# Gated scan with expert routing on one core: which queue issues the loads of gates and inputs

## The chip, the cores and the metric

The kernel runs on one core of one Trainium2 chip. The metric is the device time of one execution in microseconds (us), taken as the median of several runs. All times of single instructions below come from one profiled execution, counted from the start of its span.

## What is computed

Four sequences of 3648 tokens with 256 channels are first run through a gated linear recurrence. Each token's result then goes to one of 16 experts, chosen in two steps (a group of four, then one of its four experts), and comes back weighted. Cut to what matters:

```python
sig = 1.0 / (1.0 + np.exp(-f_logit))
f = lower_bound + (1.0 - lower_bound) * sig
h = f * h + (1.0 - f) * x[:, t]            # one step per token, h starts at 0 in each sequence
# x is now the 14592 x 256 matrix of all h
g_idx = np.argmax(x @ w_group, axis=1)     # softmax weight g_w of the winner
e_idx = np.argmax(x @ w_expert[g], axis=1) # within the group, softmax weight e_w
out = (g_w * e_w)[:, None] * (np.maximum(x @ w1[g, e], 0) @ w2[g, e])
```

## The kernel before

**Two kinds of work share the core.** The first is the scan with the routing. It goes over 29 units of 512 tokens (unit 0 to unit 28; the last has 256). For a unit the kernel loads gates and inputs in one transfer of 1 MB into a tile `zt` (`p1_load`, L157 to L170), takes the tanh on ACT (L179) and two scaled copies (L183), one product on DVE (L196) and two scans on DVE (L207). PE transposes the result (L226), computes the router's scores (L238) and transposes these (L249). DVE then finds expert and place of every token (`route_thunks`, L252 to L329; units go through it in groups of two after unit 0), with a small matmul for the counts (L284, L285) whose result DVE reads (L310). POOL scatters the tokens' rows into per-expert lists in memory (`xs`, L322).

The second is the experts' matmuls, in jobs: 16 early ones on the first tokens of each expert, 16 later ones on the rest. A job loads its tokens' rows (`xr`, L607), four pieces of weights of 512 KB (`st`, L615, five buffers), splits each piece into a 16-bit high part on ACT (`wh`, L621) and a low part on DVE (`wl`, L622), transposes the rows on PE (L636; high part L641 on ACT, low part L642 on DVE), and does the two layers on PE (L666 to L668, then L681 to L683) with the activation on ACT and DVE in between (L671, L672), a scaled copy on ACT (L687) and a scatter on POOL (L688).

**What sets the order.** The program writes both kinds of work interleaved: the scan's steps are put among a job's matmul steps so that each is done by the time that a later job is due. SyncE's queue (SP in the profile) keeps the order in which the program is written: it issues the loads of units, of rows and of weights and blank rows into the lists (L421), and each of these may wait in front of all that stand behind it. The rows of a job wait for the scatters that fill its list (L607) and for its position, which DVE computes (`posA`, L430, read by L596); a load of weights waits until one of the five buffers is free, that is for an earlier piece's L622. The other engines' orders come from a scheduler, which places each instruction by its own estimate of when it can start. All engines work through their queues in order.

**Where the loads of units stand.** The step of unit u writes the load of unit u+2, then the tanh of unit u+1 (L363). A tile `zt` has four buffers, so the load of unit u also waits for the scans of unit u-4.

```python
zt = p1.tile([P, 2, KD, UNIT], F32, name="zt", bufs=4)
seq += [lambda u=u: (p1_load(u + AHEAD - 1), u + 1 in us and p1_ta(u + 1), early_blanks(u + 4))]
```

Of the kernel before, what the change touches and what calls it, by code (L numbers as in the profile page):

```python
# [32 lines left out]
O_BUFS = 5  # L33
X_BUFS = 4
AHEAD = 3


@with_exitstack
def gated_scan_moe(ctx: ExitStack, tc, zx, lower, wroute, wexp, out, S):
    nc = tc.nc  # L40
# [101 lines left out]
    def unit_range(u):  # L142
        return u * UNIT, min(N, (u + 1) * UNIT)
# [11 lines left out]
    last_load = {}  # L155

    def p1_load(u):  # L157
        if u >= NU:
            return
        a, b = unit_range(u)  # L160
        w = b - a
        zt = p1.tile([P, 2, KD, UNIT], F32, name="zt", bufs=4)
        src = zx[u * P:(u + 1) * P, :].rearrange("p (s k w) -> p s k w", s=2, k=KD)
        if u == 0:
            for k in range(KD):
                for q in range(2):
                    nc.sync.dma_start(out=zt[:, q, k, 0:w], in_=src[:, q, k, 0:w])
        else:
            last_load[u] = nc.sync.dma_start(out=zt[:, :, :, 0:w], in_=src[:, :, :, 0:w])
        units[u] = {"z": zt}  # L170

    def p1_ta(u):
        a, b = unit_range(u)
        w = b - a
        U = units[u]
        U["h"] = p1.tile([P, KD, UNIT], F32, name="h", bufs=3)
        ff = U["z"][:, 0]
        if u > 0:
            nc.scalar.activation(ff[:, :, 0:w], U["z"][:, 0, :, 0:w], AF.Tanh, scale=0.5)  # L179
        for k in range(KD):  # L180
            if u == 0:
                nc.scalar.activation(ff[:, k, 0:w], U["z"][:, 0, k, 0:w], AF.Tanh, scale=0.5)
            nc.scalar.activation(ff[:, k, 0:w], ff[:, k, 0:w], AF.Identity, scale=hlf[:, k:k + 1],  # L183
                                 bias=cen[:, k:k + 1])
        U["f"] = ff
# [145 lines left out]
    def p1_thunks(us, groups):  # L331
# [21 lines left out]
        def put(f):  # L353
            th.append(f or (lambda: None))
            if hasattr(f, "mark"):
                marks[f.mark] = len(th)

        put(lambda: [p1_load(u) for u in range(us[0], us[0] + AHEAD - 1)])
        put(lambda: p1_ta(us[0]))
        for u in us + [us[-1] + 1]:  # L360
            seq = []
            if u in us:
                seq += [lambda u=u: (p1_load(u + AHEAD - 1), u + 1 in us and p1_ta(u + 1), early_blanks(u + 4))]  # L363
            if u - 1 in us:
# [52 lines left out]
    def early_blanks(u):  # L417
        for e, (v, n) in enumerate(EARLY):
            if v == u:
                r = e * LW + PRE - n * P  # L420
                sync.dma_start(out=xs_v[NT + e][r:r + n * P, :].rearrange("(p k) c -> p k c", k=n),  # L421
                               in_=blank[:, None, :].broadcast_to([P, n, RW]))
# [462 lines left out]
```

## Time and profile before

| what | value |
|---|---|
| median of 3 runs | 883.24 us (876.09 to 884.25) |
| profiled execution | 878.25 us |
| its span | 876.5 us |
| mean granted clock of TensorE in the span | 0.934 of full speed |
| PE busy | 753.8 us (86%) |
| DVE busy | 535.7 us (61%) |
| ACT busy | 464.2 us (53%) |
| POOL busy | 286.9 us (33%) |

PE is the engine of the matmuls, DVE the vector, ACT the scalar and POOL the general engine; SP only issues transfers. A profiled execution is 1.75 us longer than its span. Busy shares are means over the whole span, in which a first part (scan and early jobs together, up to some 390 us) and a second part (jobs alone) follow each other. In a timeline a row's bracket says how long the engine had been idle before the instruction and what ended the wait.

### The profile page before, as it was taken

What the parts mean: (1) busy time and instruction counts of PE and PEld (TensorE: products, weight loads), DVE (VectorE), ACT (ScalarE), POOL (GpSimd) and SP (SyncE); (2) the same over time, 40 slices, a digit from 0 to 9 for tenths busy, and PEclk for the clock granted to TensorE, in tenths of its full rate; (3) what the DMA queues carried; (4) which work ended last, traced back from release to release, by engine and by line L of the source; (5) the groups of instructions that cost most, each with busy time, mean ns of one, the idle gap of its engine ahead of it and who ended that gap; (6) DMA issues with size and microseconds to landing.
All of it is one profiled execution on the core that took longest, in us unless ns stands there. A gap on an engine that the chain in (4) does not pass through costs nothing.

```text
span 876.5 us, 17542 instructions
## 1 busy us (share of the span) xinstructions
PE 753.8 (86%) x6629; PEld 646.5 (74%) x6629; DVE 535.7 (61%) x1159; ACT 464.2 (53%) x808; POOL 286.9 (33%) x255
## 2 busy tenths in 40 slices
PE   3452869878887888897799999999999999999995
PEld 2231748756676776766599998999888999999895
DVE  7996959888965953672534454543656445555630
ACT  6763949588745644342545444544555445555531
POOL 0484554734634425541121121212221221112122
PEclk9665979979999989999799999999999999999998
DMA  8993999799897244247641632343543424444300
GB/s 309 273 362 124 304 295 360 225 354 323 279 255 256 101 162 161 100 163 200 223 151 43 217 105 71 105 129 90 144 138 98 122 94 150 146 151 135 126 24 22
DMA packets 59056, 155.34 MB, mean 177 GB/s; under 512 B 11179, under 2 KB 24560, under 8 KB 55515
## 3 DMA queue, kind: packets, MB, share of 16 engines
q1 hardware_dynamic: 44443, 124.12, 44.3%
q0 software_dynamic: 14240, 30.06, 9.8%
q8 instruction: 52, 0.85, 0.4%
q14 instruction: 33, 0.27, 0.1%
q10 hardware_dynamic: 288, 0.03, 0.0%
HBM read 112.65 MB, written 42.05 MB: 176 GB/s over the span
## 4 chain that ended last, share of the span: by engine, by line
PE 56%; issue 11%; DVE 9%; DMA 7%; ACT 4%; SPq 2%; POOL 2%; POOLq 0%; another core or an unknown queue 0%; DVEq 0%; ACTq 0%
PE ps_m L683 9%; PE ps_m L681 9%; PE ps_m L682 9%; PE ps_m L666 8%; PE ps_m L668 8%; PE ps_m L667 8%; DMA st<-in_wexp_dram 5%; DVE wl L622 3%; PE ps_p L636 2%; DVE hl L672 2%; ACT wh L621 2%; POOL out_dram L688 1%; SPq L488 1%; PE ps_p L238 1%; DVE h L207 1%
## 5 line engine op out<-in xcount | busy, mean ns | idle before, releaser
L688 POOL DMA_INDIRECT out_dram<-o,meta x123 | 140.9, 1146 | 472.9 <-ACT o L687 441.2
L681 PE MATMUL ps_m<-wh,hh 128*128 128x256 f16 (+6 forms) x984 | 272.6, 277 | 2.0 <-ACT o L687 1.1
L682 PE MATMUL ps_m<-wl,hh 128*128 128x256 bf16 (+6 forms) x984 | 272.4, 277 | 0.8 <-issue 0.8
L683 PE MATMUL ps_m<-wh,hl 128*128 128x256 f16 (+6 forms) x984 | 272.2, 277 | 0.9 <-issue 0.9
L666 PE MATMUL ps_m<-xh,wh 128*128 128x256 f16 (+12 forms) x896 | 252.7, 283 | 19.8 <-DVE hl L672 19.3
L672 DVE SCALAR_TENSOR_TENSOR hl<-ps_m,hh 128x512 bf16<-128x512 f32 (+11 forms) x270 | 166.1, 620 | 168.7 <-ACT hh L671 128.2
L668 PE MATMUL ps_m<-xh,wl 128*128 128x256 f16 (+12 forms) x896 | 252.4, 283 | 0.2 <-issue 0.2
L667 PE MATMUL ps_m<-xl,wh 128*128 128x256 bf16 (+12 forms) x896 | 252.4, 283 | 0.0
L671 ACT ACTIVATE hh<-ps_m 128x512 f16<-128x512 f32 (+11 forms) x270 | 146.7, 546 | 129.2 <-PE ps_m L668 112.1
L622 DVE TENSOR_TENSOR wl<-st,wh 128x1024 bf16<-128x1024 f32 x128 | 155.4, 1219 | 57.7 <-ACT wh L621 57.5
L322 POOL DMA_INDIRECT xs<-rows,posi x114 | 143.8, 1262 | 110.6 <-issue 27.7
L621 ACT CAST wh<-st 128x1024 f16<-128x1024 f32 x128 | 132.8, 1044 | 43.3 <-DMA st<-in_wexp_dram 22.8
L687 ACT ACTIVATE o<-ps_m,meta 128x256 f32<-128x256 f32 (+6 forms) x123 | 58.3, 474 | 159.5 <-PE ps_m L683 137.7
L681 PEld LDWEIGHTS <-hh 128*128 128x128 f16 (+6 forms) x984 | 112.5, 114 | 12.0 <-issue 4.1
L683 PEld LDWEIGHTS <-hl 128*128 128x128 bf16 (+6 forms) x984 | 112.4, 114 | 10.1 <-issue 2.3
L682 PEld LDWEIGHTS <-hh 128*128 128x128 f16 (+6 forms) x984 | 112.5, 114 | 9.4 <-issue 1.4
L667 PEld LDWEIGHTS <-wh 128*128 128x128 f16 x896 | 88.9, 99 | 38.0 <-issue 22.7
L666 PEld LDWEIGHTS <-wh 128*128 128x128 f16 x896 | 89.0, 99 | 19.1 <-issue 2.7
L668 PEld LDWEIGHTS <-wl 128*128 128x128 bf16 x896 | 88.8, 99 | 19.1 <-issue 1.7
L642 DVE TENSOR_TENSOR xl<-ps_p,xh 128x512 bf16<-128x512 f32 (+9 forms) x68 | 41.9, 617 | 65.1 <-ACT xh L641 64.5
L207 DVE TENSOR_TENSOR_SCAN h<-zt,h 128x512 f32<-128x512 f32 (+4 forms) x56 | 65.1, 1170 | 1.6 <-PE ps_p L226 1.4
L636 PE MATMUL ps_p<-ident,xr 128*128 128x128 f32 (+6 forms) x246 | 40.0, 284 | 30.0 <-DMA xr<-xs 22.0
(120 smaller groups left out, 506.4 us busy)
## 6 DMA issues: line engine op xcount, KB each, us to landing
st<-in_wexp_dram SPq DMA_DIRECT2D x128, 512.0 KB
zt<-in_zx_dram SPq DMA_DIRECT2D x27, 1024.0 KB
xr<-xs SPq DMA_DIRECT2D x31, 258.0 KB
xs<-blank SPq DMA_DIRECT2D x22, 258.0 KB
xr<-xs SPq DMA_DIRECT2D x8, 249.9 KB
out_dram<-o,meta POOLq DMA_INDIRECT x123
xs<-rows,posi POOLq DMA_INDIRECT x114
xs<-blank SPq DMA_DIRECT2D x3, 516.0 KB
```

What stands on the lines that cost most here:

```text
L322: sc = nc.gpsimd.indirect_dma_start(out=xs_v[G["t0"] + t][:, :], out_offset=bass.IndirectOffsetOnAxis(ap=R["posi"][:, t:t + 1], axis=0), i ...
L621: nc.scalar.copy(j.wh[i], j.st[i])
L622: nc.vector.tensor_tensor(out=j.wl[i], in0=j.st[i], in1=j.wh[i], op=ALU.subtract)
L666: nc.tensor.matmul(po, w1_at(j.wh, k, c), xh[:, k], start=(k == 0), stop=False)
L667: nc.tensor.matmul(po, w1_at(j.wh, k, c), xl[:, k], start=False, stop=False)
L668: nc.tensor.matmul(po, w1_at(j.wl, k, c), xh[:, k], start=False, stop=(k == KD - 1))
L671: nc.scalar.activation(hi, pv, AF.Relu)
L672: nc.vector.scalar_tensor_tensor(out=j.hl[ch][:, cs[0]:cs[-1] + 1, 0:w], in0=pv, scalar=0.0, in1=hi, op0=ALU.max, op1=ALU.subtract)
L681: nc.tensor.matmul(pm[0:p, 0:D], j.hh[ch][:, c, ts], w2_at(j.wh, c), start=(c == 0), stop=False)
L682: nc.tensor.matmul(pm[0:p, 0:D], j.hh[ch][:, c, ts], w2_at(j.wl, c), start=False, stop=False)
L683: nc.tensor.matmul(pm[0:p, 0:D], j.hl[ch][:, c, ts], w2_at(j.wh, c), start=False, stop=(c == KF - 1))
L688: nc.gpsimd.indirect_dma_start(out=out_v[out_n[0]][:, :], out_offset=bass.IndirectOffsetOnAxis(ap=lt[0:p, r, 0:1], axis=0), in_=o[0:p], in ...
```

## The change

Loads of unit 0 to unit 8 stay where they were; the loads of units 9 to 28 (20 transfers, nineteen of 1 MB and one of 512 KB) are issued from ACT's queue.

```diff
--- before.py
+++ after.py
@@ -33,6 +33,7 @@
 O_BUFS = 5
 X_BUFS = 4
 AHEAD = 3
+ZX_SP = 9
@@ -166,7 +167,7 @@
         else:
-            last_load[u] = nc.sync.dma_start(out=zt[:, :, :, 0:w], in_=src[:, :, :, 0:w])
+            last_load[u] = (nc.sync if u < ZX_SP else nc.scalar).dma_start(out=zt[:, :, :, 0:w], in_=src[:, :, :, 0:w])
```

Lines of the changed program are one higher (L170 is L169 before). On SP the other instructions keep their order; on ACT, DVE and PE the scheduler comes to another one.

The first place is SP's queue before and after one of the last groups of weights; `zt_3402` is unit 25, `zt_3569` unit 26, `xr` are a job's rows, `st` weights, `posA` a job's position. Before:

```order
L607 DMA xr_3291<-xs 128x516
L169 DMA zt_3402<-in_zx_dram 128x2048
L421 DMA xs<-blank_154 768x1x258 x2
L615 DMA st_3440<-in_wexp_dram 128x1024
L615 DMA st_3482<-in_wexp_dram 128x1024
L615 DMA st_3532<-in_wexp_dram 128x1024
L615 DMA st_3563<-in_wexp_dram 128x1024
L169 DMA zt_3569<-in_zx_dram 128x2048
L596 TENSOR_LOAD posA_3515
L596 ISA x2
L607 ISA
L607 DMA xr_3753<-xs 128x516
```

In the changed program the same stretch of SP reads:

```order
L608 DMA xr_3291<-xs 128x516
L422 DMA xs<-blank_154 768x1x258 x2
L616 DMA st_3440<-in_wexp_dram 128x1024
L616 DMA st_3482<-in_wexp_dram 128x1024
L616 DMA st_3532<-in_wexp_dram 128x1024
L616 DMA st_3563<-in_wexp_dram 128x1024
L597 TENSOR_LOAD posA_3515
L597 ISA x2
L608 ISA
L608 DMA xr_3753<-xs 128x516
```

The two loads of units are gone from between rows, blanks and weights.

The second place is ACT's queue around the end of one early job (`o` and `hh` are its results and activations, `ex` and `Lg` belong to the routing); `wh0_3963` and `wh1_3996` are pieces of the job whose weights are `st_3440` and `st_3482` above, `wh2_3534` and `wh3_3565` are pieces of the job ahead of it. Before:

```order
L687 ACTIVATE o_3319<-ps_m2_3294,meta_2649 128x256
L287 ACTIVATE ex_3327<-ge_3154 128x160
L250 COPY Lg_3329<-ps_p_3330 128x80
L687 ACTIVATE o_3358<-ps_m2_3333,meta_2649 128x256
L621 CAST wh0_3963<-st_3440 128x1024
L621 CAST wh2_3534<-st_3165 128x1024
L621 CAST wh1_3996<-st_3482 128x1024
L687 ACTIVATE o_3397<-ps_m2_3372,meta_2668 128x256
L621 CAST wh3_3565<-st_3193 128x1024
L671 ACTIVATE hh_3423<-ps_m1_3425 128x2x256
```

In the changed program the same place, with the load of unit 25 and the tanh of unit 24 (`zt_3131`):

```order
L170 DMA zt_3402<-in_zx_dram 128x2048
L672 ACTIVATE hh_3114<-ps_m1_3271 128x384
L688 ACTIVATE o_3319<-ps_m2_3294,meta_2649 128x256
L288 ACTIVATE ex_3327<-ge_3154 128x160
L251 COPY Lg_3329<-ps_p_3330 128x80
L688 ACTIVATE o_3358<-ps_m2_3333,meta_2649 128x256
L180 ACTIVATE zt_3131<-zt_3131 128x1024
L622 CAST wh0_3442<-st_3125 128x1024
L184 ACTIVATE zt_3131<-zt_3131,mid_85,half_83 128x512
L688 ACTIVATE o_3397<-ps_m2_3372,meta_2668 128x256
L184 ACTIVATE zt_3131<-zt_3131,mid_85,half_83 128x512
L672 ACTIVATE hh_3423<-ps_m1_3425 128x2x256
```

The load of a unit stands a few rows ahead of the tanh of the unit before it, and the casts of `st_3440` and `st_3482` have moved from here to behind the casts of all earlier pieces; in this part of the queue the casts now stand in the order of their loads, while before three of them stood ahead of older ones.

The third place is DVE's queue at the first early job's rows; `base` is the read of the routing's counts (group of units 7 and 8), `wl_886` to `wl_938` are the low parts of the first five pieces of weights, `scn` belongs to the routing, `h` to a scan. Before:

```order
L277 SCALAR_TENSOR_TENSOR scn<-rmask_403,oh_842 128x128
L196 SCALAR_TENSOR_TENSOR zt<-zt 128x1024
L207 SCALAR_TENSOR_TENSOR h<-zt,h 128x512 x2
L310 TENSOR_TENSOR base<-ps_p,runoff 128x16
L312 TENSOR_TENSOR runoff<-ps_p,runoff 128x16
L315 TENSOR_TENSOR sc<-scn,base 128x128
L642 TENSOR_TENSOR xl<-ps_p,xh 128x2x256
L644 COPY meta<-xr 128x4
```

In the changed program:

```order
L278 SCALAR_TENSOR_TENSOR scn<-rmask_403,oh_842 128x128
L197 SCALAR_TENSOR_TENSOR zt<-zt 128x1024
L311 TENSOR_TENSOR base<-ps_p,runoff 128x16
L313 TENSOR_TENSOR runoff<-ps_p,runoff 128x16
L316 TENSOR_TENSOR sc<-scn,base 128x128
L623 TENSOR_TENSOR wl_886<-st,wh_885 128x1024
L623 TENSOR_TENSOR wl_892<-st,wh_891 128x1024
L623 TENSOR_TENSOR wl_898<-st,wh_897 128x1024
L623 TENSOR_TENSOR wl_904<-st,wh_903 128x1024
L643 TENSOR_TENSOR xl<-ps_p,xh 128x2x256
L645 COPY meta<-xr 128x4
L623 TENSOR_TENSOR wl_938<-st,wh_937 128x1024
```

The five low parts, which stood some 30 to 40 rows ahead of this read, now stand behind it; so do one unit's product (unit 12) and four scans (units 11 and 12).

## Rows read from the trace of the kernel before

**Rows 1.** Windows of 50 and 200 us: busy us (instructions) of each engine, PEclk, DMA share, GB/s

```profile
250.00:300.00 50.00, 38.92 (x356) 32.41 (x355) 33.09 (x71) 29.14 (x53) 20.70 (x16) 0.93 0.68 204
500.00:700.00 200.00, 199.09 (x1759) 179.99 (x1758) 102.42 (x189) 94.80 (x168) 46.41 (x38) 1.00 0.37 113
```

**Rows 2.** Timeline of PE: start us, us, engine, line, what [idle before, releaser]

```profile
128.76 0.19 PE L284 MATMUL ps_p<-scn,tri 128*128 128x16 bf16 x1 [3.12 <-DVE scn L277]
...
181.54 0.69 PE L636 MATMUL ps_p<-ident,xr 128*128 128x128 f32 x2 [8.05 <-ACT rs L241]
...
253.13 0.27 PE L681 MATMUL ps_m<-wh,hh 128*128 128x256 f16 x1 [1.08 <-ACT o L687]
...
266.01 0.48 PE L249 MATMUL ps_p<-ident,rs 128*128 128x128 f32 x1 [4.62 <-ACT rs L241]
...
286.26 0.19 PE L284 MATMUL ps_p<-scn,tri 128*128 128x16 bf16 x1 [4.02 <-DVE xl L642]
```

**Rows 3.** Timeline of ACT, the tanh of units 18, 19, 25, 26, 27, and three casts

```profile
157.58 1.05 ACT L179 ACTIVATE zt<-zt 128x1024 f32<-128x1024 f32 x1
...
175.34 1.06 ACT L179 ACTIVATE zt<-zt 128x1024 f32<-128x1024 f32 x1 [3.68 <-DMA zt<-in_zx_dram]
...
249.88 1.06 ACT L179 ACTIVATE zt<-zt 128x1024 f32<-128x1024 f32 x1 [3.71 <-DMA zt<-in_zx_dram]
...
260.08 2.94 ACT L621 CAST wh<-st 128x1024 f16<-128x1024 f32 x3 [6.29 <-DMA st<-in_wexp_dram]
...
271.13 1.06 ACT L179 ACTIVATE zt<-zt 128x1024 f32<-128x1024 f32 x1 [4.07 <-DMA zt<-in_zx_dram]
...
281.74 1.06 ACT L179 ACTIVATE zt<-zt 128x1024 f32<-128x1024 f32 x1 [6.35 <-DMA zt<-in_zx_dram]
```

**Rows 4.** Timeline of SP's queue, loads of units 19, 26, 27 and of weights

```profile
163.89 0.42 SPq L169 DMA_DIRECT2D zt<-in_zx_dram  x1
...
243.48 19.26 SPq L615 DMA_DIRECT2D st<-in_wexp_dram  x4
262.79 0.42 SPq L169 DMA_DIRECT2D zt<-in_zx_dram  x1
...
275.98 0.42 SPq L169 DMA_DIRECT2D zt<-in_zx_dram  x1
```

**Rows 5.** Chain that ended last, in order of time: start us, us, what

```profile
165.13 13.96 DMA st<-in_wexp_dram
```

**Rows 6.** Windows of 5 us and less, columns as in rows 1

```profile
155.00:160.00 5.00, 5.00 (x59) 4.29 (x58) 5.00 (x13) 3.74 (x7) 4.09 (x4) 1.00 0.26 96
175.00:180.00 5.00, 0.00 (x0) 0.00 (x0) 3.08 (x6) 3.43 (x5) 3.89 (x4) 0.72 1.03 355
180.00:185.00 5.00, 3.46 (x18) 2.61 (x19) 3.78 (x6) 4.17 (x8) 0.00 (x0) 0.50 1.02 411
265.00:270.00 5.00, 3.99 (x21) 2.99 (x22) 5.00 (x7) 2.06 (x6) 4.09 (x4) 0.66 0.94 353
...
286.20:290.00 3.80, 2.91 (x15) 1.87 (x14) 3.74 (x6) 3.80 (x9) 1.74 (x2) 0.55 0.55 164
```

**Rows 7.** Lines L169 and L82: duration in ns, min/median/max, of one issue

```profile
L169 SPq DMA_DIRECT2D zt<-in_zx_dram x28: 327/424/1407, 2.6 to 277.9; - x28
L82 ACTq DMA_DIRECT2D wr<-in_wroute_dram x1: 473/473/473, 1.2 to 1.2; - x1
```

**Rows 8.** Timeline of DVE around the first early job

```profile
55.03 1.21 DVE L622 TENSOR_TENSOR wl<-st,wh 128x1024 bf16<-128x1024 f32 x1
...
78.43 2.46 DVE L207 TENSOR_TENSOR_SCAN h<-zt,h 128x512 f32<-128x512 f32 x2
85.26 0.17 DVE L310 TENSOR_TENSOR base<-ps_p,runoff 128x16 f32<-128x16 f32 x1 [4.37 <-PE ps_p L285]
...
116.31 0.69 DVE L642 TENSOR_TENSOR xl<-ps_p,xh 128x512 bf16<-128x512 f32 x1 [5.08 <-ACT xh L641]
...
127.14 1.23 DVE L196 SCALAR_TENSOR_TENSOR zt<-zt 128x1024 f32<-128x1024 f32 x1 [5.02 <-ACT zt L183]
```

## The prediction

> **What bounds the kernel now.** I read four views in this order: windows by stage, the timeline of PE for its idle times, the timelines of ACT and SP for what ended them, and the chain of waits at the worst place. The windows show two kernels in one. From 500 to 700 us PE is busy 199.09 of 200 us at full clock, and nothing but PE's own work sets the time there; from 250 to 300 us, where scan and early jobs run together, it is busy 38.92 of 50 us at a clock of 0.93 [rows 1]. PE's order from the middle of that part on is the same in both programs, so what PE gains before some 300 us should arrive at the end nearly whole, and the change touches nothing later.
>
> The reader is then to look for the idle times of PE in that part. Five of them matter here [rows 2]: 3.12 us at 128.76, 8.05 at 181.54, 1.08 at 253.13, 4.62 at 266.01 and 4.02 at 286.26. After a longer one the granted clock is low (0.50 from 180 to 185, 0.66 from 265 to 270, 0.55 from 286.2 to 290) [rows 6], so each costs more than its length: what PE was busy there times one minus the clock.
>
> The timeline of ACT says what they waited for [rows 3]. The tanh of units 19, 25, 26 and 27 stood 3.68, 3.71, 4.07 and 6.35 us for their loads, and three casts in a row at 260.08 stood 6.29 us for weights. SP's queue says why those loads were late [rows 4]: unit 26 was issued at 262.79, right behind four loads of weights that took SP 19.26 us to get rid of because they wait for free buffers, and unit 27 at 275.98, behind the rows of a job that wait for scatters.
>
> **The change part by part.** SP loses 20 issues of 0.42 us [rows 7]; it mostly waits, so this alone is worth nothing. ACT gains 20, and each now leaves a few rows ahead of the tanh of the unit before.
>
> *Casts at 260.08.* The first of these is `wh0_3963`, whose weights SP began to issue at 243.48 [rows 4]; it belongs to the job after the next one, yet stands in ACT's queue ahead of a piece that PE needs sooner. ACT held the routing's copy `rs` back for it, and PE stood 4.62 us [rows 2]. In the changed order this cast comes later and those in its place have weights loaded earlier. Gain 4.62 + 3.99 x 0.34 = 6.0 us [rows 2, 6]. Bounds: nothing, if another wait fills the place, and 6.0. I take 6.0, since the order alone removes it.
>
> *Unit 27.* Its load will leave ahead of the tanh of unit 26, which without its own wait can start at 271.13 - 4.07 = 267.1. It took 281.74 - 275.98 = 5.8 us from issue to tanh, so it lands at 272.9; ACT asks for it at 281.74 - 6.35 = 275.4 [rows 3, 4]. Covered by 2.5 us, the wait goes, and with it PE's 4.02 us and 2.91 x 0.45 = 1.3 us of clock: 5.3 us [rows 2, 6]. Bounds 0 and 5.3. I take 5.3. The load of unit 26 leaves ahead of the tanh of unit 25 (249.88 - 3.71 = 246.2, 16.6 us sooner), and that of unit 25 sooner too: PE's 1.08 us at 253.13 goes as well.
>
> *Unit 19.* PE's 8.05 us do not end with the tanh but with the cast behind it, whose weights were issued at 165.13 and took 13.96 us [rows 5]; unit 19's 1 MB stood right ahead of them (163.89) [rows 4]. It will leave ahead of the tanh of unit 18, at about 157.6 [rows 3], where the transfer engines are busy only 0.26 [rows 6]. 1 MB less in front at 355 GB/s is 3.0 us. Bounds: nothing, if unit 20's load takes its place beside the weights, and 8.05 + 3.46 x 0.5 = 9.8 us if the whole stall goes. I take 3.0; the 3.68 us of the tanh lie under the weights' wait. The weights are late next.
>
> *ACT's own cost.* 20 x 0.47 us (the nearest row of an issue by ACT, of a small transfer) = 9.4 us of ACT's queue [rows 7]. ACT is busy 29.14 of 50 us in the first row of rows 1, so much of this falls into its waits. Behind an issue stand a tanh and the activations that PE's next products need. Bounds 0 and 9.4; I take 2, for a fifth of it, as PE is idle in about a fifth of that window.
>
> *First early job.* The five low parts, one product and four scans come to stand behind DVE's read at 85.26, which waits for PE [rows 8]: 5 x 1.21 + 1.23 + 2 x 2.46 = 12.2 us of DVE work put off. The cover is DVE's later idling, 5.08 us before 116.31 and 5.02 before 127.14 [rows 8]. Left over: 12.2 - 10.1 = 2.1 us. The first job's products wait for the first four parts, 4 x 1.21 = 4.8 us, but the second pair of jobs waits for its rows anyway. Bounds: a gain of 3.1 (the stall at 128.76, where the count now stands ahead of the next unit's product on DVE, goes and nothing is left over) and a loss of 12.2. I take a loss of 2.1.
>
> Sum: -6.0 - 5.3 - 1.1 - 3.0 + 2.0 + 2.1 = -11.3 us. Against the profiled execution this is 878.25 - 11.3 = 867.0 us. The runs' median, 883.24, lies 5.0 above that execution, which gives 871.9; I forecast 869, the middle of the two. Rivals below are put on the same middle, 880.7 for no change.
>
> A rule speaks against all this. The Trainium skill's page "DMA: Bandwidth & Descriptors", in "Issuing engines are not separate DMA queues", says that transfers of all issuing engines run on the same 16 engines and that spreading them saves only issue time, small beside the transfer. By it the terms of units 19 and 27 would be zero, which is the first rival. The rows of SP agree on the size of an issue (0.42 us) but show a load held 19.26 us by its place in the queue, which that sentence leaves out.
>
> **The rivals.** *No change that can be seen.* The transfer engines are the limit: from 175 to 185 us they are busy 1.03 and 1.02 of the time [rows 6], and a unit that leaves sooner only delays the weights. Then the terms of units 19, 25 and 27 go, and 6.0 of the casts less 4.1 of costs remain: 880.7 - 1.9 = 879. Against it: the share is 0.26 at 155 to 160, so there is room in which to go sooner [rows 6].
>
> *Slower.* The bound in the first part is the in-order pair ACT and DVE. From 85 us on DVE carries the 12.2 us put off and ACT the 9.4 us of issues; the scatters, and so the rows of every early job, come later by both. Nothing removes it but the 6.0 of the casts: 880.7 + 12.2 + 9.4 - 6.0 = 896. It decides if DVE does not idle between 105 and 130 us any more and is still behind at 130; it turns into a loss once the two costs pass the 15.4 us of the gains. For it: the five parts stand right in front of the first products. Against: the 10.1 us of idle time that DVE has there [rows 8].
>
> *More.* The stall at 181.54 goes whole (9.8 instead of 3.0) and the one at 128.76 too (gain 3.1 instead of a loss of 2.1): 869 - 6.8 - 5.2 = 857. For it: both waits hang on units whose loads now leave by themselves. Against: the weights at 165.13 have more than 1 MB ahead of them.
>
> **How the numbers follow.** Forecast 0.48, no change 0.23, slower 0.15, more 0.14. A difference of 1%, 8.8 us, is about what a measurement can tell from none; it lies at 871.9. The forecast's own range is 862 to 876 (about half of the gains more or less), of which some seven tenths lie below: 0.34. Faster by over 1%: 0.34 + 0.14 = 0.48. Within 1%: 0.14 of the forecast and 0.22 of the first rival: 0.36. Slower: 0.15 and 0.01 of that rival: 0.16. The range is 853 to 890: it leaves out the end of the third rival and most of the second.
>
> **What would show it.** Right: PE's idle times at the places of 253, 266 and 286 us gone, the tanh of units 25 to 27 without waits, three casts no longer in a row behind 6 us of waiting, the low clock after them gone; the first products of the first job about 5 us later, and DVE without its waits of 5 us near 116 and 127. Wrong: casts waiting for weights as long as the tanh did before (the first rival), or the second pair's rows, which DVE takes at 116.31 [rows 8], more than 6 us later and the lead still lost at 200 us (the second). The forecast fails altogether if ACT's issues wait long in its queue, because everything behind them then waits too.

## The result, and the profile after

| what | before | after |
|---|---|---|
| median | 880.28 us (4 runs, 876.09 to 884.25) | 854.32 us (4 runs, 852.42 to 854.65) |
| profiled execution | 878.25 us | 852.42 us |
| granted clock, whole span | 0.934 | 0.951 |
| PE busy | 753.8 us | 742.5 us |

The medians are 26.0 us apart, and the ratio is 0.9686 with an interval of 0.9656 to 0.9715. The prediction had said 869 us, 11.3 us less: the direction was right, the size less than half. Beside other kernels on other chips the changed kernel came to 0.9727 and 0.9695.

The windows of after, with the columns of [rows 1]. The stretch from 200 to 250 us of before was not shown yet and stands ahead.

Before:

```profile
200.00:250.00 50.00, 43.29 (x351) 31.57 (x349) 45.86 (x89) 35.82 (x65) 23.95 (x18) 0.97 0.87 296
```

After:

```profile
200.00:250.00 50.00, 49.20 (x423) 37.82 (x422) 48.91 (x102) 39.45 (x73) 27.34 (x23) 1.00 0.96 299
250.00:300.00 50.00, 48.07 (x476) 41.41 (x473) 40.94 (x84) 31.66 (x58) 22.83 (x19) 1.00 0.71 247
300.00:350.00 50.00, 40.66 (x335) 32.72 (x336) 29.69 (x92) 21.85 (x44) 27.43 (x26) 0.90 0.38 125
500.00:700.00 200.00, 199.09 (x1761) 180.74 (x1759) 103.95 (x186) 96.78 (x170) 44.95 (x37) 1.00 0.37 112
```

From 500 to 700 us nothing has changed, as foreseen. From 200 to 300 us PE stood idle 100 - 43.29 - 38.92 = 17.8 us and now 100 - 49.20 - 48.07 = 2.7 us, and its clock rose from 0.97 and 0.93 to full.

SP's queue gives the lead of the changed kernel at points that both programs reach: each row is the issue of a job's rows (`xr`). Before:

```profile
161.05 1.84 SPq L607 DMA_DIRECT2D xr<-xs  x2
...
211.81 0.92 SPq L607 DMA_DIRECT2D xr<-xs  x2
...
274.16 1.77 SPq L607 DMA_DIRECT2D xr<-xs  x2
...
312.30 1.53 SPq L607 DMA_DIRECT2D xr<-xs  x3
...
384.44 3.93 SPq L607 DMA_DIRECT2D xr<-xs  x6
```

After, the same jobs:

```profile
158.08 0.89 SPq L608 DMA_DIRECT2D xr<-xs  x2
...
207.95 1.26 SPq L608 DMA_DIRECT2D xr<-xs  x2
...
261.53 0.95 SPq L608 DMA_DIRECT2D xr<-xs  x2
...
290.78 1.26 SPq L608 DMA_DIRECT2D xr<-xs  x3
...
357.48 4.22 SPq L608 DMA_DIRECT2D xr<-xs  x6
```

The lead is 3.0, 3.9, 12.6, 21.5 and 27.0 us. So, by these rows, 17.7 of the 25.8 us between the two profiled executions arise between 210 and 310 us.

PE's idle times of [rows 2] are gone or small. So is one of 6.74 us that [rows 2] does not list. Before:

```profile
114.57 1.08 PE L636 MATMUL ps_p<-ident,xr 128*128 128x128 f32 x4 [6.74 <-DMA xr<-xs]
```

The timeline of PE after, at this place, at 181 us, at its first idle time of over 1 us behind 200 us, and at the end of the first part:

```profile
114.88 0.63 PE L637 MATMUL ps_p<-ident,xr 128*128 128x128 f32 x4 [0.84 <-DMA xr<-xs]
...
180.12 0.44 PE L637 MATMUL ps_p<-ident,xr 128*128 128x128 f32 x2 [1.11 <-ACT rs L242]
...
302.00 0.33 PE L250 MATMUL ps_p<-ident,rs 128*128 128x128 f32 x1 [2.11 <-ACT rs L242]
...
395.37 0.48 PE L667 MATMUL ps_m<-xh,wh 128*128 128x384 f16 x1 [14.48 <-DVE hl L673]
```

The 8.05 us at 181.54 are 1.11, and between 200 and 300 us nothing over 1 us is left. The last row is not new, but it is 4.5 us longer than its counterpart before and takes so much of the lead back:

```profile
421.11 0.48 PE L666 MATMUL ps_m<-xh,wh 128*128 128x384 f16 x1 [9.94 <-DVE hl L672]
```

ACT after, with the load of unit 26 and the tanh of units 25, 26 and 27, which answer to [rows 3], and the longest wait of a cast there:

```profile
246.55 0.33 ACTq L170 DMA_DIRECT2D zt<-in_zx_dram  x1
248.01 1.08 ACT L180 ACTIVATE zt<-zt 128x1024 f32<-128x1024 f32 x1
...
259.46 1.06 ACT L180 ACTIVATE zt<-zt 128x1024 f32<-128x1024 f32 x1
...
268.23 1.10 ACT L180 ACTIVATE zt<-zt 128x1024 f32<-128x1024 f32 x1
...
298.09 1.04 ACT L622 CAST wh<-st 128x1024 f16<-128x1024 f32 x1 [8.67 <-DMA st<-in_wexp_dram]
```

None of these three waits, and the three casts behind 6.29 us are gone. Up to here every sign that the prediction had named for the casts and for units 25 to 27 is there. Only the experiments show that the causes it gave were mostly the wrong ones.

### The profile page after: what moved, and what is told of

The parts are those of the page before. It is cut to its first block, busy times and chain, and to the rows that moved or that the text cites. A ratio compares the mean times of both kernels' runs of the same rounds, so it can differ in the third digit from the quotient of the medians.

```text
span 850.3 us, 17541 instructions
## 1 busy us (share of the span) xinstructions
PE 742.5 (87%) x6629; PEld 639.9 (75%) x6629; DVE 539.9 (63%) x1159; ACT 459.8 (54%) x808; POOL 283.1 (33%) x255
## 4 chain that ended last, share of the span: by engine, by line
PE 54%; issue 12%; DVE 8%; DMA 8%; ACT 3%; POOL 3%; SPq 2%; POOLq 0%; another core or an unknown queue 0%; DVEq 0%; ACTq 0%
PE ps_m L683 9%; PE ps_m L682 9%; PE ps_m L684 9%; PE ps_m L667 8%; PE ps_m L669 8%; PE ps_m L668 8%; DMA st<-in_wexp_dram 5%; DVE wl L623 2%; PE ps_p L637 2%; POOL out_dram L689 2%; DVE h L208 1%; POOL xs L323 1%; SPq L489 1%; DMA xs<-rows,posi 1%; ACT wh L622 1%
## 5 line engine op out<-in xcount | busy, mean ns | idle before, releaser
L682 PE MATMUL ps_m<-wh,hh 128*128 128x256 f16 (+6 forms) x984 | 269.6, 274 | 3.0 <-issue 1.8
L683 PE MATMUL ps_m<-wl,hh 128*128 128x256 bf16 (+6 forms) x984 | 269.6, 274 | 0.9 <-issue 0.6
L323 POOL DMA_INDIRECT xs<-rows,posi x114 | 139.6, 1224 | 131.3 <-issue 27.8
L682 PEld LDWEIGHTS <-hh 128*128 128x128 f16 (+6 forms) x984 | 111.4, 113 | 13.1 <-issue 4.4
L227 PE MATMUL ps_p<-ident,h 128*128 128x128 f32 x228 | 43.9, 321 | 12.2 <-DVE h L208 11.4
```

The costliest lines, as they stand in the source:

```text
L323: sc = nc.gpsimd.indirect_dma_start(out=xs_v[G["t0"] + t][:, :], out_offset=bass.IndirectOffsetOnAxis(ap=R["posi"][:, t:t + 1], axis=0), i ...
L682: nc.tensor.matmul(pm[0:p, 0:D], j.hh[ch][:, c, ts], w2_at(j.wh, c), start=(c == 0), stop=False)
L683: nc.tensor.matmul(pm[0:p, 0:D], j.hh[ch][:, c, ts], w2_at(j.wl, c), start=False, stop=False)
```

## The experiments

The change does two things at once: it moves 20 loads to another queue, and it makes the scheduler write ACT, DVE, PE and POOL in another order. To part them, a kernel can be given any order of both programs. When all is written, each instruction of an engine is tied to the one ahead of it in a table, for issue order alone (in short):

```diff
+    for eng, names in ORDER.items():
+        last = None
+        for n in names:
+            i = traced.get(n)
+            if last is not None:
+                tc.add_manual_dep(i, last.name, NoSync, reason="order")
+            last = i
```

The tables are read from the built programs. With this, *order alone* has all loads on SP and the other engines in the order of after; *queue alone* has the loads on ACT and all else in the order of before. Two more give the stage. No run pins an unchanged order; *casts_alone* below, at 1.0009, is the nearest to one. Each run has one profile, and the only one of before comes from the first group of runs, so a difference of a few us between before and an experiment in single windows or waits may be that of two chips. Times and ratios are against before in the same group.

```diff
 late_units:   ZX_SP = 19
 early_units:  (nc.scalar if 9 <= u < 19 else nc.sync)
```

> All loads of units stay on SP's queue at their places of before; the order of ACT, DVE, PE and POOL is pinned to that of the changed program. Queue theory (the gain comes from the loads leaving SP's queue): within 1% of before, 872 to 889 us. Order theory (the gain comes from the scheduler's other order): 850 to 860 us. The prediction's own split, 6.0 us for the casts by order and 2.1 lost on the first job: 876 us.

> The loads of units 9 to 28 go to ACT's queue, while ACT (but for the loads), DVE, PE and POOL keep the order of before, the three casts ahead of older ones included. Queue theory: 850 to 862 us. Order theory: 875 us or more. If both parts are needed together: between, 862 to 875 us.

> Only the loads of units 19 to 28 go to ACT's queue. By the times at which jobs' rows are issued in the two traces the lead is 3.0 us at 158 us, where unit 19 is loaded, and 27.0 us in the end: if each load earns its part where it stands, this one has 24 of the 27.7 us, 856 us. If the gain is an even share per load (10 of 20), 866 us. If relief of the first part is what all rests on, 875 us or more.

> Only the loads of units 9 to 18 go to ACT's queue. Lead by place: 3 to 4 us, 876 us. Even share per load: 866 us. If all rests on the first part: 857 us or less. A loss (over 884 us) if ACT's issues and the first job's order cost more than they bring.

| run | time, us | ratio to before | interval |
|---|---|---|---|
| order_alone | 857.23 | 0.9784 | 0.9711 to 0.9858 |
| queue_alone | 871.57 | 0.9939 | 0.9904 to 0.9974 |
| late_units | 853.69 | 0.9757 | 0.9677 to 0.9837 |
| early_units | 887.73 | 1.0171 | 1.0103 to 1.0240 |

(before 876.55 us in these.) The order brings most without one load moved, and the queue little without the new order. The change to units from 19 on carries the gain; loads of units 9 to 18 on ACT with the rest left on SP, in the order that the scheduler then makes, cost 11 us between the medians (1.0 to 2.4%). In that kernel the tanh of units 22 to 28 have only 43, 51, 54, 60, 68, 71 and 73 activations of jobs ahead of them on ACT, and stand 23.3 us for their loads from 200 to 330 us. What ACT waited for from 100 to 330 us tells why the queue alone is not enough (columns: us in all, times, longest). Before:

```profile
ACT zt L179 <- DMA zt<-in_zx_dram: 18.3, 5, 6.3
...
ACT wh L621 <- DMA st<-in_wexp_dram: 10.5, 4, 6.3
```

Queue alone:

```profile
ACT wh L622 <- DMA st<-in_wexp_dram: 20.2, 10, 6.3
```

The tanh no longer waits for loads at all, and the casts wait for weights longer, 20.2 us against 10.5: of 28.8 us of ACT's waits in these two rows 20.2 are left. That is the first rival's picture.

**Casts out of turn.** The prediction had taken 6.0 us for the casts at 260.08, two of which (`wh0_3963`, `wh1_3996`) stand ahead of older ones; an earlier cast does so too. In *casts_alone* these three and their low parts trade places so that all stand in the order of their loads; nothing else moves (7 places on ACT, 7 on DVE). On ACT, for instance:

```
 L687 ACTIVATE o_3358<-ps_m2_3333,meta_2649 128x256
+L621 CAST wh2_3534<-st_3165 128x1024
+L621 CAST wh3_3565<-st_3193 128x1024
 L621 CAST wh0_3963<-st_3440 128x1024
-L621 CAST wh2_3534<-st_3165 128x1024
+L687 ACTIVATE o_3397<-ps_m2_3372,meta_2668 128x256
 L621 CAST wh1_3996<-st_3482 128x1024
-L687 ACTIVATE o_3397<-ps_m2_3372,meta_2668 128x256
-L621 CAST wh3_3565<-st_3193 128x1024
```

*after_inverted* does the reverse in the changed kernel, *casts_queue* adds the loads on ACT to casts_alone.

> Before, every engine in its own order of before, all loads on SP's queue; only the three casts that stand ahead of older ones (and their low parts) change places with these, so that casts and low parts stand in the order of their loads: 7 places on ACT and 7 on DVE. Theory casts (these three places carry most of what order alone brought, 0.978): 0.975 to 0.985 of before. The prediction's term, 6.0 us: 0.993. Theory rest (routing ahead of the next unit's work, the first job's low parts, PE's order carry it): 0.99 to 1.00.

> After, with the 20 loads on ACT's queue and every engine in its order of after; only casts and low parts stand in the mutual order of before again (the same 7 places on ACT and on DVE). Theory casts: the gain falls from 27 us to about 8, ratio 0.985 to 1.00. The prediction's term: 0.969 + 6.0 us = 0.975. Theory rest: 0.97 or less.

> Before's order on all engines but for the casts and low parts in the order of their loads, and the loads of units 9 to 28 on ACT's queue: the two parts together without the rest of the new order. If casts (0.978) and queue (0.994) add up and nothing else matters: 0.97 to 0.975, like after. If the rest of the order carries the gain: 0.985 to 0.995.

> The changed kernel once more, beside the three others on one chip: 0.966 to 0.972 of before.

| run | time, us | ratio to before | interval |
|---|---|---|---|
| casts_alone | 863.76 | 1.0009 | 0.9979 to 1.0038 |
| after_inverted | 848.16 | 0.9821 | 0.9785 to 0.9858 |
| casts_queue | 855.34 | 0.9910 | 0.9880 to 0.9941 |
| after_again | 839.75 | 0.9727 | 0.9690 to 0.9764 |

(before 863.77 us.) In the order of before the places of the three casts are worth nothing; in that of after the same places cost 848.16 - 839.75 = 8.4 us. The waits of ACT in casts_alone from 200 to 330 us show what came in their place:

```profile
ACT zt L179 <- DMA zt<-in_zx_dram: 21.9, 3, 10.6
```

Before, the same row of the same stretch had 14.1 us:

```profile
ACT zt L179 <- DMA zt<-in_zx_dram: 14.1, 3, 6.3
```

The wait moved from the casts to the tanh. So the theory that these casts carry the order's gain falls.

**Which part of the order.** *late_order* has the order of before up to 168 us and that of after from there on. The three others keep the order of before and move one class of instructions to where after has it, as far as the order of all pairs on which both programs agree is kept. All loads stay on SP.

> All loads on SP's queue. Every engine stands in its order of before up to the first cast behind which unit 19 was loaded (168 us in the trace of before), and in its order of after from there on. Theory late order: the later part alone carries what order brings, ratio 0.975 to 0.985. Theory first job (low parts and scans put off at 85 us fill DVE's idle time from 100 to 150 us, and all rests on that): 0.995 or more. Half and half: 0.988.

> All loads on SP's queue, orders of before; only the units' own work (tanh and scaled copies on ACT, product and scans on DVE) stands among the rest where after has it, as far as the dependences both orders share allow; it mostly comes later. Theory units (they ran ahead of what was due and stood in front of it): 0.978 to 0.987. Else 0.995 to 1.005; and over 1.005 if late scans hold up PE's transposes.

> All loads on SP's queue, orders of before; only the routing's steps (maxima, places, positions and rows on DVE, the exponential on ACT, the counts on PE) stand among the rest where after has them; they mostly come earlier. Theory routing (positions and rows sooner, so the next jobs' rows are loaded sooner): 0.978 to 0.987. Else 0.995 to 1.005.

> All loads on SP's queue, orders of before; only casts on ACT and low parts on DVE stand among the rest where after has them: in the order of their loads, mostly later and one by one between the activations of a job instead of in bursts. Theory spread casts (a burst of casts and low parts stands in front of activations that PE waits for): 0.978 to 0.987. Else 0.995 to 1.005, as the mere change of places gave 1.001.

| run | time, us | ratio to before | interval |
|---|---|---|---|
| late_order | 859.45 | 0.9754 | 0.9704 to 0.9804 |
| units_moved | 866.25 | 0.9838 | 0.9784 to 0.9891 |
| routing_moved | 877.65 | 0.9945 | 0.9909 to 0.9980 |
| casts_moved | 890.78 | 1.0102 | 1.0070 to 1.0135 |

(before 882.33 us.) The later part of the order carries all of its gain, as far as the intervals tell (0.9754 here, 0.9784 for the whole order). Within it the units' own work is the largest piece that was tried, routing a small one, and the new places of the casts cost time by themselves.

**Which units, and the queue once more.** *last_eight* moves only the own work of units 21 to 28, *order_again* repeats order_alone beside the changed kernel, and *after_old_casts* puts the casts of the changed kernel where before has them. In last_eight ACT's order changes like this around the tanh of unit 23 (`zt_2908`; `hh` and `o` belong to a job):

```
-L179 ACTIVATE zt_2908<-zt_2908 128x1024
-L183 ACTIVATE zt_2908<-zt_2908,mid_85,half_83 128x512 x2
 L687 ACTIVATE o_3068<-ps_m2_3043,meta_2363 128x256
 L228 COPY rows_2944<-ps_p_3073 128x2x256
+L687 ACTIVATE o_3104<-ps_m2_3079,meta_2370 128x256
+L250 COPY Lg_2875<-ps_p_3111 128x80
+L671 ACTIVATE hh_3114<-ps_m1_3116 128x384
+L179 ACTIVATE zt_2908<-zt_2908 128x1024
```

> The order of after with all loads on SP's queue, once more, beside the changed kernel on one chip. If the queue adds what it gave to the order of before (0.994) or to that with casts in place (0.990): 0.975 to 0.98 of before here, and the changed kernel 5 to 9 us less. If the queue adds nothing once the order is right: the two alike within 3 us.

> The changed kernel, for comparison with order_again: 0.967 to 0.973 of before.

> All loads on SP's queue, orders of before; only the own work of units 21 to 28 (tanh, scaled copies, product, scans) stands where after has it. On ACT the tanh of units 22 to 28 then have 49, 56, 64, 70, 73, 78 and 80 activations of jobs ahead of them instead of 45, 53, 56, 62, 69, 71 and 73. Theory late units (ACT asked for the last loads too early and stood): 0.980 to 0.988, what all units moved gave. If the earlier units carry it: 0.995 or more.

> The changed kernel with 20 loads on ACT's queue and its order, but casts and low parts standing among the rest where before has them, out of turn ones included, as far as the dependences both orders share allow. Moved alone, the new places of casts cost 1.0%. If that adds up: 0.957 to 0.965, better than both. As the out-of-turn casts cost the changed kernel 1.0% (after_inverted), it may cancel: 0.97. If casts must stand late where the units do: 0.98 or more.

| run | time, us | ratio to before | interval |
|---|---|---|---|
| order_again | 841.76 | 0.9744 | 0.9704 to 0.9784 |
| after_third | 837.68 | 0.9695 | 0.9657 to 0.9734 |
| last_eight | 851.57 | 0.9861 | 0.9819 to 0.9902 |
| after_old_casts | 844.66 | 0.9783 | 0.9743 to 0.9823 |

(before 864.88 us.) On one chip the order brings 864.88 - 841.76 = 23.1 us and the queue on top of it 841.76 - 837.68 = 4.1 us. Eight units, moved behind 1 to 8 more activations of jobs, bring 13.3 us. The windows of last_eight, columns as in [rows 1]:

```profile
200.00:250.00 50.00, 45.49 (x385) 34.72 (x383) 45.08 (x101) 33.71 (x63) 25.37 (x20) 0.97 0.92 303
250.00:300.00 50.00, 48.03 (x480) 41.91 (x479) 45.96 (x85) 37.15 (x67) 30.83 (x23) 1.00 0.58 212
```

PE is busy 48.03 us from 250 to 300 instead of 38.92 [rows 1], the same as in after, with every load still on SP's queue. Of the idle times that the prediction had priced there, the two of over 4 us are gone. The longest one left waits for DVE's part of a job's activation:

```profile
236.74 0.32 PE L666 MATMUL ps_m<-xh,wh 128*128 128x384 f16 x1 [2.70 <-DVE hl L672]
```

Three like it stood before, where the prediction did not price them:

```profile
214.93 0.32 PE L666 MATMUL ps_m<-xh,wh 128*128 128x384 f16 x1 [1.31 <-DVE hl L672]
...
237.37 0.32 PE L666 MATMUL ps_m<-xh,wh 128*128 128x384 f16 x1 [3.22 <-DVE hl L672]
...
290.53 0.28 PE L666 MATMUL ps_m<-xh,wh 128*128 128x256 f16 x1 [1.36 <-DVE hl L672]
```

The wait of a tanh for a load, 14.1 us of before, is no longer among ACT's waits from 200 to 330 us; its longest for a transfer is now for weights:

```profile
ACT wh L621 <- DMA st<-in_wexp_dram: 11.3, 2, 11.1
```

The old places of the casts make the changed kernel 7 us slower, though the new ones are a loss in the old order: parts of an order are not worth the same in another one.

**As a plain edit.** *pin_tanh* orders nothing by table. It ties the tanh of units 21 to 28 to its place in the written program, with all loads on SP. *later_still* is the changed kernel with the tanh written a step later, which also tries for a better one.

```diff
 pin_tanh:
-            nc.scalar.activation(ff[:, :, 0:w], U["z"][:, 0, :, 0:w], AF.Tanh, scale=0.5)
+            (tc.keep_in_program_order if u > 20 else (lambda i: i))(nc.scalar.activation(ff[:, :, 0:w], U["z"][:, 0, :, 0:w], AF.Tanh, scale=0.5))
 later_still:
-   seq += [lambda u=u: (p1_load(u + AHEAD - 1), u + 1 in us and p1_ta(u + 1), early_blanks(u + 4))]
+   seq += [lambda u=u: (p1_load(u + AHEAD - 1), early_blanks(u + 4))]
-   seq += [lambda u=u: p1_tb(u, 1)]
+   seq += [lambda u=u: (p1_tb(u, 1), u + 1 in us and p1_ta(u + 1))]
```

> Before with one edit: the tanh of units 21 to 28 may not stand ahead of anything that is written before it on ACT; all loads stay on SP's queue and the scheduler orders the rest. The tanh of units 22 to 28 then have 49, 53, 66, 69, 72, 76 and 88 activations of jobs ahead of them (before 45, 53, 56, 62, 69, 71, 73; after 49, 56, 65, 70, 73, 78, 80). Theory asked too early: 0.983 to 0.990, as last_eight gave 0.986. If it was the loads that had to leave sooner: 0.995 or more.

> The changed kernel, with the tanh of the next unit written at the end of a unit's step instead of its start; the loads stay on ACT's queue. On ACT the tanh of units 22 to 28 have 54, 62, 68, 72, 77, 80 and 83 activations of jobs ahead of them (after: 49, 56, 65, 70, 73, 78, 80), those of units 14 to 21 four to seven more than in after too. If later is better still: 0.960 to 0.967. If after already asks late enough and more lateness only holds up the scans, the routing and the next jobs' rows: 0.972 to 0.99.

pin_tanh took 854.60 us, 0.9902 (0.9864 to 0.9939) of before's 861.75; later_still 841.89 us, 0.9770 (0.9726 to 0.9813). The plain edit brings 7 us, just outside of what was expected (0.983 to 0.990). In its waits from 200 to 330 us the tanh is out of the way, but the casts wait more than in last_eight:

```profile
ACT wh L621 <- DMA st<-in_wexp_dram: 20.5, 9, 5.5
...
ACT zt L179 <- DMA zt<-in_zx_dram: 1.4, 1, 1.4
```

Still later brought nothing more: 0.9770, beside 0.9686, 0.9727 and 0.9695 of the changed kernel in other groups. The intervals overlap with that of 0.9727, and the two were not run in one group, so that later is worse was not shown. None of the runs beat the changed kernel by its ratio.

## Why the prediction was right or wrong

**What holds.** The gain is in the first part, arrives at the end nearly whole, and PE's idle times and the low clock behind them are where it comes from. That the forecast had the right sign is in part luck: most of its terms gave a wrong cause, as follows.

**The step that failed: what the new order of the engines is worth, against what the loads' leaving sooner is worth.** In the prediction's sum the order stands with 6.0 us for the casts less 2.1 for the first job, 3.9 us, and the queue with 5.3 + 1.1 + 3.0 - 2.0 = 7.4 us. On one chip the order measured 23.1 us and the queue 4.1. The new places of the units' own work, the largest piece of the order that was tried, have no term beyond the first job.

**Units 25 and 27 (6.4 us), "Its load will leave ahead of the tanh of unit 26".** The load does leave there, and the wait does go. But sending sooner is not what paid most. With the same loads sent by ACT in the old order the tanh stops waiting too, and the time falls by 5 us (queue_alone). With the loads left on SP and the own work of the last eight units placed later, it falls by 13.3 us (last_eight), near the 12.4 that the prediction had put on the idle times at 253, 266 and 286 us. So these idle times were priced about right, and another cure is enough for them: to put the tanh, and the scaled copies, product and scans that hang on it, behind more of a job's activations. The front part shows a row of this that the prediction passed over: at its second place the changed order of ACT holds the tanh of unit 24 (`zt_3131`), where the old one has no tanh any more, since that of unit 25 already stood ahead of it.

**Casts (6.0 us, "the order alone removes it").** Nothing by their own places: 1.0009. The stall was there, but the wait behind it, a tanh's, took its place (21.9 us instead of 14.1). The lower bound, zero, was right. In the order of after the same three places do cost 8.4 us.

**Unit 19 (3.0 us, "1 MB less in front").** The stall went nearly whole, 8.05 to 1.11 us, as the third rival had it, but not because weights came sooner. In the chain of waits after, the weights issued at 165.67 took 0.8 us less than the 13.96 us of [rows 5], not 3.0:

```profile
165.67 13.16 DMA st<-in_wexp_dram
```

In order_alone the stall is gone as well, with unit 19 on SP; the longest idle time of PE between 160 and 260 us there is below 1.5 us.

**ACT's cost (2.0 us).** An issue on ACT took less than the nearest row had said, 334 ns instead of 473:

```profile
L170 ACTq DMA_DIRECT2D zt<-in_zx_dram x20: 334/334/632, 35.9 to 264.8; - x20
```

The queue with its cost is worth 4.1 us net in the new order (order_again to after_third), 5 us and 8.4 us in the old one (queue_alone; casts_alone to casts_queue); the prediction had 7.4. Cost and benefit were not parted further.

**First job (2.1 us lost).** DVE's waits of 5.08 and 5.02 us near 116 and 127 us are gone, as said: from 100 to 150 us DVE is busy 48.79 us instead of 39.84. The first products did not come 5 us later, they came at 83.34 instead of 85.83 us. From the first job's transposes (84.08 and 80.94 us) to the rows at 161.05 and 158.08 the lead stays at 3 us: the 6.74 us of idle time at 114.57 go, but PE stands idle 15.7 us in this stretch after and 13.1 before, so others came in their place. The first part of the order is worth nothing that can be told from zero: late_order, without it, gains as much (0.9754) as the whole order (0.9744 and 0.9784, with intervals of 0.4 to 0.7% to either side). The slower rival, which rested on it, did not come true.

**The sum.** The prediction priced five idle times of PE and the clock for a few us behind each. In the stretch from 200 to 300 us that gave 9.7 us of idle time and 2.7 of clock. The windows of the same stretch hold 17.8 us of idle time, and clock for 43.29 x 0.03 + 38.92 x 0.07 = 4.0 us; 15.1 and all 4.0 of these went, 19.1 us, against 17.7 us of lead. The idle time that the prediction put at nothing is 17.8 - 9.7 = 8.1 us. Of these 5.9 lie in three gaps longer than the shortest one it priced (1.08 us): 3.22 us at 237.37, 1.36 at 290.53 and 1.31 at 214.93, all ended by DVE's part of a job's activation (`hl`). The prediction gives no reason for leaving them out. Only some 2 us lay in shorter gaps.

**The rivals.** "No change" was right on its own point: moving the queue alone leaves 0.6%, and in its trace the casts wait for weights longer. The rule of the Trainium skill's page "DMA: Bandwidth & Descriptors", section "Issuing engines are not separate DMA queues", by which spreading transfers over issuing engines saves little, fits the queue's part of the result (0.5 to 1.0%). It doesn't speak of the instructions whose order changes with the issuing engine, and those carried 23 of the 27 us. "More", at 857 us, was nearest in size, and both of its stalls did go (8.05 to 1.11 us at 181.54, and none in front of the count that stood at 128.76). Its nearness is luck all the same: the first goes without any load moved (order_alone), and the first part of the order, where the second lies, is worth nothing that can be told from zero.

**What stays open.** Units moved bring 1.6%, routing 0.6% and casts cost 1.0%, while the whole order brings 2.2 to 2.6%: the parts do not add up, and the places of the jobs' own instructions were not tried alone. Nor is it settled how much of the units' 13.3 us is the tanh's waiting and how much its mere work in front of a job's. Less waiting for transfers can't be all of it: in pin_tanh ACT waits for them 20.5 + 1.4 = 21.9 us from 200 to 330 us, not less than before (14.1 + 6.3 = 20.4), and is 7 us faster. Nor is it known why PE's wait at the end of the first part grew from 9.94 to 14.48 us.

## What to carry to other kernels

When a transfer moves to an engine whose order a scheduler sets, compare the order of every instruction that depends on it, not only what stands around the issue: here the queue was worth 4 us and the new order 23, of which 13 came with the later places of eight units' work alone. A wait for a load can go by asking later as well as by sending sooner, and here asking later paid more. Price a stage by the idle time and clock of its whole window, and use a list of stalls to learn causes; a stall that is taken away alone can be replaced by the one queued behind it, as in casts_alone.

## What the runs showed of the hardware

The same program before took 861.75 to 882.33 us (medians) in the five groups of experiments, each on a chip of its own, 2.4% apart, while ratios to before of the same group repeated better: the changed kernel gave 0.9686, 0.9727 and 0.9695 in three groups. A difference of a few microseconds between groups says nothing.

Weights of 512 KB took 13 to 14 us from issue to landing around 165 us both with 1 MB of a unit right ahead of them on the same queue and without (13.96 and 13.16 us), while the transfer engines' share from 150 to 200 us rose from 0.90 to 0.99. Before and after, in that order:

```profile
150.00:200.00 50.00, 39.84 (x348) 31.84 (x346) 43.05 (x88) 34.04 (x59) 28.90 (x23) 0.90 0.90 299
150.00:200.00 50.00, 44.34 (x401) 35.08 (x399) 49.21 (x98) 38.48 (x69) 33.42 (x25) 0.97 0.99 332
```

So here, taking the 1 MB out from in front of the weights did not bring them 3 us sooner.
